# A fused attention and two feed-forward layers: weight sums at conversion, token forms on two engines, and a new order of copies in ScalarE's row

## The chip, the cores and the metric

The kernel runs on one core of a Trainium2 chip. What counts is the device time of one execution, in microseconds, as the median of several runs. A core has five engines that run side by side, each through a row of its own instructions in order: TensorE (PE; matmuls, with its weight loads shown as PEld), VectorE (DVE), ScalarE (ACT), GpSimd (POOL) and SyncE (SP), which only starts transfers here. They wait for each other through semaphores. Matmuls write to PSUM, a memory of eight banks of 128 x 512 numbers here; everything else lies in SBUF.

## What is computed

A decaying linear attention over blocks of 64 positions, then two feed-forward layers on 1536 tokens of width 512. In the reference:

```python
x = attn_out.transpose(0, 2, 1, 3).reshape(B * S, H * D)   # 1536 x 512
h = x @ w_in                                               # 512 -> 2048
g = np.where(h >= 1, h, np.where(h <= -1, 0.0, (h + 1) ** 2 / 4))
x = g @ w_out                                              # 2048 -> 512
gate = 1.0 / (1.0 + np.exp(-(x @ w_gate)))                 # 512 -> 1536
val = x @ w_val                                            # 512 -> 1536
return (gate * val @ w_out2).astype(np.float32)            # 1536 -> 512
```

Everything is float32. The weights come as 64-bit words.

## The kernel before

**Precision.** TensorE takes numbers of a shorter type (fp32r). So each operand is split in two, a high part and the rest, and each product is made of three matmuls: high times high, low times high, high times low. A split is a copy on ScalarE (to the short type) and a subtraction on VectorE (the rest).

**Stages.** Attention fills the first 80 us or so. Then comes the first layer: 16 slices of 128 hidden units, three blocks of 512 tokens. GROUPS cuts the 16 slices in groups (4, 3, 3, 3, 3); for a group, each block is taken in turn, and for each slice of the group there are 12 matmuls of `hidden` and 12 of `project`. A unit is one slice on one block. `feed_forward` issues the `project` of a unit two units later (LAG = 2). At a group's last slice `flush` (L239) adds the four banks of sums to `part[t]` on VectorE; after the last group it also splits the result into `xh` and `xl` (L247, L248), the tokens of the second layer.

**The second layer** has 12 slices, each with a gate and a value. For the first two token blocks, gate and value of a slice are 2 x 2 blocks of weights times tokens, and they are computed with 7 block products and not 8, as in Strassen's method. This needs sums of token blocks (token forms, `x_forms`) and sums of weight blocks (`w_forms`), which are then split too (L323 and L324 for tokens; `w_forms_split` with L346 on ScalarE and L347 on GpSimd for weights). The third token block is computed plainly by `single`. `pair_begin` and `pair_end` make the seven products of a slice (6 matmuls each, L357, in banks p0, p1, p2). p0 gathers several products one after the other: each time that its value is one of the results, ScalarE copies it out (L374, L378, L382), and the next product adds on top. The next product into p0 must wait for that copy.

**An iteration** of `second_layer` takes two slices n0 and n1 (GF = 2): the pair of n0 (its first five products, then the waiting projects of the last iteration, then its last two), the pair of n1, and the projects and singles: 204 matmuls, 180 in the first iteration, which has no waiting projects, while the last two projects come after the sixth.

**Weights.** Pieces of 128 x 512 weights come in by DMA and are converted by `w_round`, a pipeline of three steps for three pieces: words (L99, L100 on ScalarE), float (L106, L107, L109 on VectorE), high and low part (L113 on ScalarE, L117 on VectorE). NWP = 10 tiles hold converted pieces. `w_forms` of before takes high and low of two pieces, adds them to whole numbers (L335, two additions on GpSimd per slice), and makes four half-size sums (L339).

**What sets the order.** The program is written in the order in which each engine runs it. There is no scheduler that moves instructions: what stands earlier in the code on an engine runs earlier. Work for a later step, as conversions and splits, is called between the products. `later` is a list of splits that `finish` takes one at a time after a project. Tiles of a pool with n buffers are reused in turn; a write into a reused buffer waits for the last reader of its old content. `rest` tiles are r and q, `parts` makes gh and gl, the split of the activations (L185, L186).

Of the kernel before, what the change touches and what calls it, by code (L numbers as in the profile page):

```python
# [17 lines left out]
P = 128  # L18
# [7 lines left out]
GROUPS = (4, 3, 3, 3, 3)  # L26
GF = 2
# [11 lines left out]
def fused_kernel(ctx: ExitStack, tc: tile.TileContext, qkv, qd, cst, w1, w2, out):  # L39
# [9 lines left out]
    gp = ctx.enter_context(tc.tile_pool(name="gp", bufs=5))  # L49
# [28 lines left out]
    raws, ws, tmps = {}, {}, {}  # L78

# [14 lines left out]
    def w_words(i):  # L94
        word = raws[i].bitcast(U32).rearrange("p (n two) -> p n two", two=2)
        lo, hi = word[:, :, 0], word[:, :, 1]
        r = tp.tile([P, 512], F32, tag="r", bufs=3, name=f"wr{i}")
# [17 lines left out]
    def w_low(i, eng):  # L115
        r = tmps.pop(i)[1]
        eng.tensor_tensor(out=ws[i][:, 1], in0=r, in1=ws[i][:, 0].bitcast(F32), op=ALU.subtract)  # L117
# [3 lines left out]
    def w_round(eng=dve, between=None, low=dve):  # L121
        k = prog["round"]
# [17 lines left out]
        if 0 <= k - 2:  # L140
            w_low(k - 2, low)
        if eng is dve:
            w_load()
# [35 lines left out]
    def rest(name):  # L179
        return gp.tile([P, TT], F32, tag="r", name=name)  # L180
# [76 lines left out]
    def feed_forward(rounds):  # L257
# [14 lines left out]
        for u in seq:  # L272
# [14 lines left out]
            if n == NF1 - 1 and t == 1:  # L287
                w_need(NF1, 0)
                w_need(NF1, 512)
                w_forms(NF1)  # L290
                later.append(lambda: w_forms_split(NF1))
# [15 lines left out]
    forms = {}  # L307
    xt = {}

    def x_forms():  # L310
# [7 lines left out]
        for o, a, b_ in ((x1, y1, x1), (y1, y2, y1), (y2, y2, x1), (x2, x2, y2)):  # L318
            pool.tensor_tensor(out=o, in0=a, in1=b_, op=ALU.subtract)
# [6 lines left out]
        for i in (1, 0, 3, 2):  # L326
            later.append(lambda i=i: split(i))

    def w_forms(n):

        hw = HK * P
        v, g = f = [gv.tile([P, 512], F32, tag="gv", name=f"{c}{n}") for c in "vg"]
        for o, d in ((512, v), (0, g)):
            w = ws[index[n, o]]
            pool.tensor_tensor(out=d, in0=w[:, 0].bitcast(F32), in1=w[:, 1].bitcast(F32), op=ALU.add)  # L335
        v1, v2, g1, g2 = v[:, 0:hw], v[:, hw:], g[:, 0:hw], g[:, hw:]
        for o, a, b_, op in ((v2, v1, v2, ALU.add), (v1, g1, v1, ALU.subtract),
                             (g1, v2, g1, ALU.subtract), (g2, g2, g1, ALU.subtract)):
            pool.tensor_tensor(out=o, in0=a, in1=b_, op=op)  # L339
        forms[n] = f  # L340

    def w_forms_split(n):
        tiles = []
        for i, f in enumerate(forms[n]):
# [63 lines left out]
    def second_layer():  # L408
        waiting = []
        for n0 in range(NF1, NF1 + NF2, GF):  # L410
# [27 lines left out]
            if n2 < NF1 + NF2:  # L438
                w_forms_split(n2)
# [376 lines left out]
```

## Time and profile before

| | us |
| --- | --- |
| median of 3 runs | 683.87 |
| lowest and highest run | 683.08, 684.03 |
| the profiled execution, its time | 681.24 |
| span of the profiled execution | 679.5 |

| stage (us of the span) | length | matmuls in the program |
| --- | --- | --- |
| 80 to 319.64, first layer | 239.64 | 1057 records |
| 319.64 to 345.50, its end after the second block | 25.86 | 48 |
| 345.50 to 395.07, slices 16 and 17 | 49.57 | 180 |
| 395.07 to 447.94, slices 18 and 19 | 52.87 | 204 |
| 447.94 to 503.97, slices 20 and 21 | 56.03 | 204 |
| 503.97 to 560.91, slices 22 and 23 | 56.94 | 204 |
| 560.91 to 618.33, slices 24 and 25 | 57.42 | 204 |
| 618.33 to 675.19, slices 26 and 27, with the last two projects | 56.86 | 228 |

The profile is that of one execution, whose time is 2.63 us under the median. In its rows, a tile's name has its buffer number left out, `<-` reads as "made from", and a bracket at the end of a timeline row gives the idle time just before it and what ended it. PEclk is the clock that TensorE was granted, as a share of 2.4 GHz.

### The profile page before, as it was taken

To read this page: it belongs to the slowest core of one execution; us is meant where nothing else is said; L and a number is where in the kernel's file an instruction comes from. 1 tells how busy PE (TensorE), PEld (TensorE's weight loads), DVE (VectorE), ACT (ScalarE), POOL (GpSimd) and SP (SyncE) were. 2 spreads that over 40 slices of the span, in tenths; PEclk is the share of its full clock that TensorE was granted. 3 is DMA by queue.
4 is the path that set the end of the run, shared out by engine and by line. 5 is a ranking of instruction groups with operands and counts; after the bars stand their busy time and mean duration, and the time that the engine had idled before them with its cause. 6 is when DMAs were issued, how large, how long until landed. Compare 5 with 4: busy or idle time off the path is not lost.

```text
span 679.5 us, 8022 instructions
## 1 busy us (share of the span) xinstructions
PE 621.5 (91%) x3004; PEld 499.5 (74%) x3004; DVE 436.2 (64%) x699; ACT 329.7 (49%) x593; POOL 164.5 (24%) x158
## 2 busy tenths in 40 slices
PE   8889899999999999999478997996997899699897
PEld 5767688888888888888366876874876687488686
DVE  6665832676675685697786884596398279353344
ACT  6667644665564563655454564434353254222220
POOL 4367500000000000043904054052232405404100
PEclk8999899999999999999778998998999799699899
DMA  8965300132130121231021321132033012000013
GB/s 283 359 237 188 123 31 1 63 97 90 61 94 32 63 93 32 63 93 32 7 87 32 110 82 56 32 93 63 0 94 93 1 62 63 0 0 1 1 55 130
DMA packets 15813, 52.58 MB, mean 77 GB/s; under 512 B 1688, under 2 KB 2976, under 8 KB 15776
## 3 DMA queue, kind: packets, MB, share of 16 engines
q1 hardware_dynamic: 15760, 52.08, 23.3%
q8 instruction: 23, 0.38, 0.2%
q14 instruction: 14, 0.11, 0.0%
q10 hardware_dynamic: 16, 0.01, 0.0%
HBM read 48.92 MB, written 3.15 MB: 77 GB/s over the span
## 4 chain that ended last, share of the span: by engine, by line
PE 55%; issue 19%; POOL 10%; DVE 7%; ACT 6%; DMA 2%; SPq 1%; POOLq 0%
PE a L217 24%; PE h L163 8%; PE h L165 8%; PE h L164 8%; PE p L357 6%; POOL s L347 3%; POOL v L339 2%; POOL g L335 2%; POOL g L339 2%; DVE pT L630 1%; POOL v L335 1%; DMA u<-in_qkv 1%; ACT wr L99 1%; DVE xl L687 1%; DMA pd<-pw 1%
## 5 line engine op out<-in xcount | busy, mean ns | idle before, releaser
L217 PE MATMUL a<-gh,w 128*128 128x512 f32 x384 | 121.8, 399 | 5.1 <-ACT gh L185 5.1
L163 PE MATMUL h<-xh,w 128*128 128x512 f32 x288 | 112.6, 391 | 0.3 <-ACT xh L686 0.3
L165 PE MATMUL h<-xl,w 128*128 128x512 f32 x288 | 112.2, 390 | 0.0
L164 PE MATMUL h<-xh,w 128*128 128x512 f32 x288 | 112.2, 389 | 0.0
L217 PE MATMUL a<-w,gh 128*128 128x512 f32 x288 | 89.1, 391 | 1.2 <-DVE part L239 1.2
L217 PEld LDWEIGHTS a<-gh,w 128*128 128x128 f32 x384 | 74.2, 194 | 21.0 <-ACT gh L185 5.5
L217 PE MATMUL a<-gl,w 128*128 128x512 f32 x192 | 76.9, 401 | 5.0 <-DVE gl L186 5.0
L198 DVE SCALAR_TENSOR_TENSOR r<-r,h 128x512 f32<-128x512 f32 x48 | 32.9, 685 | 74.4 <-ACT r L194 74.4
L193 ACT ACTIVATE r<-h,half 128x512 f32<-128x512 f32 x48 | 33.1, 689 | 87.7 <-PE h L165 87.7
L239 DVE TENSOR_TENSOR part<-part,a 128x512 f32<-128x512 f32 x108 | 67.8, 680 | 7.3 <-PE a L217 7.3
L335 POOL TENSOR_TENSOR v<-w 128x512 f32<-128x512 f32 x12 | 17.5, 1458 | 215.1 <-DVE w L117 215.1
L347 POOL TENSOR_TENSOR s<-v,s 128x512 fp32r<-128x512 f32 x12 | 15.8, 1319 | 217.6 <-ACT s L346 144.5
L357 PE MATMUL p<-xth,s 128*128 128x512 f32 x96 | 40.3, 498 | 30.0 <-ACT q L374 25.5
L217 PEld LDWEIGHTS a<-w,gh 128*128 128x128 f32 x288 | 53.8, 188 | 13.8 <-DVE part L239 2.5
L163 PEld LDWEIGHTS h<-xh,w 128*128 128x128 f32 x288 | 54.1, 188 | 12.1 <-ACT xh L686 0.7
L165 PEld LDWEIGHTS h<-xl,w 128*128 128x128 f32 x288 | 54.0, 188 | 11.6 <-DVE xl L687 0.3
L164 PEld LDWEIGHTS h<-xh,w 128*128 128x128 f32 x288 | 54.1, 188 | 11.1
L185 ACT ACTIVATE gh<-r 128x512 fp32r<-128x512 f32 x60 | 37.5, 625 | 48.0 <-DVE r L403 35.5
L186 DVE TENSOR_TENSOR gl<-r,gh 128x512 fp32r<-128x512 f32 x60 | 43.0, 717 | 20.5 <-ACT gh L185 20.5
L217 PE MATMUL a<-w,gl 128*128 128x512 f32 x144 | 56.1, 389 | 0.0
L107 DVE SCALAR_TENSOR_TENSOR wr<-raw,wr 128x512 uint32<-128x512 uint32 x68 | 54.4, 799 | 2.3
L357 PEld LDWEIGHTS p<-xth,s 128*128 128x128 f32 x96 | 22.0, 234 | 41.2 <-ACT q L374 30.1
(97 smaller groups left out, 1083.1 us busy)
## 6 DMA issues: line engine op xcount, KB each, us to landing
raw<-in_w SPq DMA_DIRECT2D x68, 512.0 KB, 3.5
u<-in_qkv SPq DMA_DIRECT2D x12, 768.0 KB, 5.6
u<-in_qkv SPq DMA_DIRECT2D x8, 384.0 KB, 6.3
out<-part SPq DMA_DIRECT2D x12, 256.0 KB, 2.1
DT<-pd SPq DMA_DIRECT2D x1, 256.0 KB, 4.6
qp<-pd SPq DMA_DIRECT2D x2, 96.0 KB, 4.6
DT<-pd SPq DMA_DIRECT2D x1, 128.0 KB
cs<-in_cst SPq DMA_DIRECT2D x1, 98.0 KB, 2.0
```

The source lines that it names most:

```text
L107: dve.scalar_tensor_tensor(out=ru, in0=hi, scalar=0x80000000, in1=ru, op0=ALU.bitwise_and, op1=ALU.bitwise_or)
L163: pe.matmul(h, lhsT=wh, rhs=xh[:, k, tt], start=(k == 0), stop=False)
L164: pe.matmul(h, lhsT=wl, rhs=xh[:, k, tt], start=False, stop=False)
L165: pe.matmul(h, lhsT=wh, rhs=xl[:, k, tt], start=False, stop=(k == NP - 1))
L185: act.activation(gh, g, AF.Copy)
L186: dve.tensor_tensor(out=gl, in0=g, in1=gh.bitcast(F32), op=ALU.subtract)
L193: act.activation(r, h, AF.Relu, bias=half, scale=0.5)
L217: pe.matmul(accs[j], lhsT=a, rhs=b_, start=(first and m == 0), stop=(last and m == 2))
L239: dve.tensor_tensor(out=o, in0=o, in1=accs[j], op=ALU.add)
L335: pool.tensor_tensor(out=d, in0=w[:, 0].bitcast(F32), in1=w[:, 1].bitcast(F32), op=ALU.add)
L347: pool.tensor_tensor(out=t[:, 1], in0=f, in1=t[:, 0].bitcast(F32), op=ALU.subtract)
L357: pe.matmul(o, lhsT=a, rhs=b_, start=(start and k == 0 and m == 0), stop=(k == HK - 1 and m == 2), skip_group_check=True)
```

## The change

1. `w_forms` is called from `w_round` right behind the low part of a slice's second piece, and works in place on the whole numbers that the conversion has (tile r of `w_words`, now five buffers); the two additions L335 are not there any more. The forms are split in the next `w_round`, ScalarE and GpSimd as before. So a slice's forms are made and split a group ahead. The pool fp of split forms has four buffers, not three; the pool gv is gone.
2. `x_forms` makes two of the four token forms on VectorE and two on GpSimd, and the splits of two forms are in one step of `later`.
3. GROUPS is (4, 3, 3, 2, 4), and gh and gl have four buffers, not five.
4. A pair is a generator. The last two products of the first pair come behind the waiting projects as before; then each step of the second pair (up to its fifth product) comes with one step of the first pair's activation parts behind it, so the copies of the second pair's p0 stand ahead of the parts in ScalarE's row. The parts of the second pair stand between the two `hidden` of a `single`, the parts of a single behind the next project. `w_round` is called in front of each waiting project, eight times per iteration in all.

The diff, cut to its core:

```diff
-GROUPS = (4, 3, 3, 3, 3)
+GROUPS = (4, 3, 3, 2, 4)
...
+    def w_forms(i):
+        n, o = pieces[i]
         r = tmps.pop(i)[1]
+        whole[n, o] = r
+        if n < NF1 or o != 512:
+            return
+        hw = NP // 2 * P
+        v, g = whole.pop((n, 512)), whole.pop((n, 0))
+        v1, v2, g1, g2 = v[:, 0:hw], v[:, hw:], g[:, 0:hw], g[:, hw:]
+        for o, a, b_, op in ((v2, v1, v2, ALU.add), (v1, g1, v1, ALU.subtract),
+                             (g1, v2, g1, ALU.subtract), (g2, g2, g1, ALU.subtract)):
+            pool.tensor_tensor(out=o, in0=a, in1=b_, op=op)
+        forms[n] = v, g
...
     def w_round(eng=dve, between=None, low=dve):
+        split = [n for n in forms if n not in ready]
+        w_steps(eng, between, low)
+        for n in split:
+            w_forms_split(n)
+
+    def w_steps(eng, between, low):
...
             w_low(k - 2, low)
+            w_forms(k - 2)
...
-        for o, a, b_ in ((x1, y1, x1), (y1, y2, y1), (y2, y2, x1), (x2, x2, y2)):
-            pool.tensor_tensor(out=o, in0=a, in1=b_, op=ALU.subtract)
+        for eng, o, a, b_ in ((dve, x1, y1, x1), (pool, y1, y2, y1), (dve, y2, y2, x1),
+                              (pool, x2, x2, y2)):
+            eng.tensor_tensor(out=o, in0=a, in1=b_, op=ALU.subtract)
...
-        for i in (1, 0, 3, 2):
+        later.append(lambda: (split(0), split(1)))
+        later.append(lambda: None)
+        for i in (3, 2):
             later.append(lambda i=i: split(i))
...
+    def pair_act(n, r, gs):
+        hi, lo = ([gp.tile([P, TT], F32R, tag=c, name=f"{c}{n}_{t}") for t in range(2)]
+                  for c in ("gh", "gl"))
+        gs.update({t: (hi[t], lo[t]) for t in range(2)})
+        rest_of = lambda t: dve.tensor_tensor(out=lo[t], in0=r[t], in1=hi[t].bitcast(F32),
+                                              op=ALU.subtract)
+        act.activation(hi[0], r[0], AF.Copy)
+        yield
+        rest_of(0)
+        act.activation(r[1], r[1], AF.Sigmoid)
+        yield
+        dve.tensor_tensor(out=r[1], in0=r[1], in1=r[2], op=ALU.mult)
+        yield
+        act.activation(hi[1], r[1], AF.Copy)
+        yield
+        rest_of(1)
+        yield
...
-            a = pair_begin(n0)
-            w_need(n1, 0)
-            w_need(n1, 512)
-            w_forms(n1)
+            a, b = pair(n0), pair(n1)
+            for _ in range(5):
+                next(a)
             for p in waiting:
+                w_round()
                 project(*p)
-                w_round()
-            ga = pair_end(*a)
-            w_forms_split(n1)
-            w_round()
-            b = pair_begin(n1)
+            ra, ga = next(a), {}
+            xa = pair_act(n0, ra, ga)
+            for _ in range(5):
+                next(b)
+                next(xa)
             w_round()
             project(n0, 0, ga[0], True, False)
             w_round()
-            gb = pair_end(*b)
-            w_round()
-            ha = single(n0, 2)
+            rb, gb = next(b), {}
+            ha = single(n0, 2, pair_act(n1, rb, gb))
             w_round()
             project(n1, 0, gb[0], False, True)
...
+            ha = parts(ha, n0, 2)
             w_round()
             hb = single(n1, 2)
...
-    fp = ctx.enter_context(tc.tile_pool(name="fp", bufs=3, reuse_waits="tile"))
-    gv = ctx.enter_context(tc.tile_pool(name="gv", bufs=2, reuse_waits="tile"))
+    fp = ctx.enter_context(tc.tile_pool(name="fp", bufs=4, reuse_waits="tile"))
```

How the rows of the engines change is shown at three places. Names end in slice numbers (q20_1 is the copy 1 of slice 20; s22_1 a split form of slice 22) or in piece numbers (w52, wr54, raw54: pieces of weights; 50 and 51 are slice 22's). The first is ScalarE's row in the iteration of slices 20 and 21, between the two pairs. Before:

```order
L113 ACTIVATE w53_3933<-wr53_3813 128x512
L99 ACTIVATE wr55_3935<-raw55_3912 128x512
L100 ACTIVATE wc55_3936<-raw55_3912 128x512
L185 ACTIVATE gh20_0_3956<-q20_0_3839 128x512
L393 ACTIVATE q20_1_3840<-q20_1_3840 128x512
L185 ACTIVATE gh20_1_3962<-q20_1_3840 128x512
L346 ACTIVATE s21_0_3966<-v21_3878 128x512
L346 ACTIVATE s21_1_3969<-g21_3879 128x512
L374 ACTIVATE q21_0_3975<-p21_0_3972 128x512
L378 ACTIVATE q21_1_3976<-p21_0_3972 128x512
L379 ACTIVATE q21_0_3975<-q21_0_3975 128x512
```

In the kernel with the change, from the first pair's sigmoid on:

```order
L398 ACTIVATE q20_0_3830<-q20_0_3830 128x512
L140 ACTIVATE s22_0_3869<-wr51_3727 128x512
L140 ACTIVATE s22_1_3872<-wr50_3689 128x512
L114 ACTIVATE w52_3894<-wr52_3768 128x512
L100 ACTIVATE wr54_3896<-raw54_3825 128x512
L101 ACTIVATE wc54_3897<-raw54_3825 128x512
L385 ACTIVATE q21_0_3936<-p21_0_3933 128x512
L413 ACTIVATE gh20_0_3946<-q20_0_3830 128x512
L416 ACTIVATE q20_1_3831<-q20_1_3831 128x512
L391 ACTIVATE q21_1_3937<-p21_0_3933 128x512
L420 ACTIVATE gh20_1_3947<-q20_1_3831 128x512
```

The copies q21_0 and q21_1 stood behind gh20_0, gh20_1 and two splits; now q21_0 stands ahead of gh20_0 and q21_1 ahead of gh20_1, and the splits are those of slice 22, ahead of the conversion of w52 and the words of piece 54.

The second is VectorE's row at the same place, from the last flush addition of the waiting projects on. Before:

```order
L239 TENSOR_TENSOR part2_1014<-part2_1014,a18_2_3_3898 128x512
L106 TENSOR_SCALAR wr54_3907<-wr54_3907 128x512
L107 SCALAR_TENSOR_TENSOR wr54_3907<-raw54_3818,wr54_3907 128x512
L109 ISA wr54_3907<-wr54_3907,wc54_3908 128x1024
L117 TENSOR_TENSOR w53_3933<-wr53_3813,w53_3933 128x512
L390 TENSOR_TENSOR q20_0_3839<-q20_0_3839,p20_0_3836 128x512
L391 TENSOR_TENSOR q20_1_3840<-q20_1_3840,p20_2_3838 128x512
L186 TENSOR_TENSOR gl20_0_3957<-q20_0_3839,gh20_0_3956 128x512
L394 TENSOR_TENSOR q20_1_3840<-q20_1_3840,q20_2_3841 128x512
L186 TENSOR_TENSOR gl20_1_3963<-q20_1_3840,gh20_1_3962 128x512
L376 TENSOR_TENSOR q21_0_3975<-q21_0_3975,p21_1_3973 128x512
```

With the change:

```order
L272 TENSOR_TENSOR part2_1011<-part2_1011,a18_2_3_3887 128x512
L401 TENSOR_TENSOR q20_0_3830<-q20_0_3830,p20_0_3827 128x512
L403 TENSOR_TENSOR q20_1_3831<-q20_1_3831,p20_2_3829 128x512
L388 TENSOR_TENSOR q21_0_3936<-q21_0_3936,p21_1_3934 128x512
L411 TENSOR_TENSOR gl20_0_3948<-q20_0_3830,gh20_0_3946 128x512
L418 TENSOR_TENSOR q20_1_3831<-q20_1_3831,q20_2_3832 128x512
L397 TENSOR_TENSOR q21_2_3938<-q21_2_3938,p21_2_3935 128x512
L411 TENSOR_TENSOR gl20_1_3949<-q20_1_3831,gh20_1_3947 128x512
```

One conversion (of pieces 53 and 54) that stood between the flush and the multiplication into q20_0 is gone from here, and the first addition of slice 21 (q21_0) stands ahead of gl20_0.

The third is VectorE's row in the transition from the first layer to the second, from the last flush addition of the second token block on (part1). Before:

```order
L239 TENSOR_TENSOR part1_1013<-part1_1013,a13_1_3_2844 128x512
L248 TENSOR_TENSOR xl_77<-part1_1013,xh_76 128x512 x2
L324 TENSOR_TENSOR xtl_1016<-part1_1013,xth_1015 128x1024
L186 TENSOR_TENSOR gl14_2_2956<-r14_2_2912,gh14_2_2955 128x512
L198 SCALAR_TENSOR_TENSOR r15_2_2959<-r15_2_2959,h15_2_0_2942 128x512
L324 TENSOR_TENSOR xtl_1016<-part0_79,xth_1015 128x1024
L106 TENSOR_SCALAR wr37_2804<-wr37_2804 128x512
L107 SCALAR_TENSOR_TENSOR wr37_2804<-raw37_2752,wr37_2804 128x512
L109 ISA wr37_2804<-wr37_2804,wc37_2805 128x1024
L117 TENSOR_TENSOR w36_2984<-wr36_2747,w36_2984 128x512
L186 TENSOR_TENSOR gl15_2_2994<-r15_2_2959,gh15_2_2993 128x512
L324 TENSOR_TENSOR xl_77<-part1_1013,xh_76 128x2x512
```

With the change (L347 are the token forms, L352 their splits):

```order
L272 TENSOR_TENSOR part1_1010<-part1_1010,a12_1_3_2761 128x512
L281 TENSOR_TENSOR xl_77<-part1_1010,xh_76 128x512 x2
L347 TENSOR_TENSOR part0_79<-part1_1010,part0_79 128x1024
L347 TENSOR_TENSOR part1_1010<-part1_1010,part0_79 128x1024
L352 TENSOR_TENSOR xtl_1013<-part0_79,xth_1012 128x1024
L352 TENSOR_TENSOR xtl_1013<-part1_1010,xth_1012 128x1024
L219 TENSOR_TENSOR gl13_2_2894<-r13_2_2848,gh13_2_2893 128x512
L231 SCALAR_TENSOR_TENSOR r14_2_2897<-r14_2_2897,h14_2_0_2880 128x512
L107 TENSOR_SCALAR wr35_2633<-wr35_2633 128x512
L108 SCALAR_TENSOR_TENSOR wr35_2633<-raw35_2593,wr35_2633 128x512
L110 ISA wr35_2633<-wr35_2633,wc35_2634 128x1024
L118 TENSOR_TENSOR w34_2920<-wr34_2588,w34_2920 128x512
```

Two forms of 1024 columns came to VectorE, the two splits of the first forms stand ahead of gl13_2, and since the last group has four slices, one unit more follows.

## Rows read from the trace of the kernel before

**Rows 1.** The page's busy table: busy us, share of the span, instructions.
```profile
PE 621.5 (91%) x3004; PEld 499.5 (74%) x3004; DVE 436.2 (64%) x699; ACT 329.7 (49%) x593; POOL 164.5 (24%) x158
```

**Rows 2.** Windows by stage: length; busy us (instructions) per engine; PEclk, DMA share, GB/s.
```profile
80.00:319.64 239.64, 239.64 (x1057) 198.42 (x1056) 155.27 (x250) 134.01 (x227) 11.98 (x10) 1.00 0.20 64
319.64:345.50 25.86, 15.71 (x50) 11.56 (x49) 22.02 (x22) 10.37 (x16) 18.30 (x10) 0.77 0.12 33
345.50:395.07 49.57, 44.16 (x182) 35.17 (x181) 37.61 (x56) 30.23 (x52) 9.69 (x10) 0.95 0.24 71
395.07:447.94 52.87, 49.01 (x206) 39.26 (x204) 34.18 (x51) 24.35 (x44) 16.72 (x16) 0.97 0.19 57
447.94:503.97 56.03, 49.39 (x206) 39.21 (x205) 37.55 (x55) 22.86 (x41) 17.77 (x17) 0.94 0.19 57
503.97:560.91 56.94, 50.29 (x205) 39.86 (x204) 37.56 (x55) 22.84 (x41) 17.79 (x17) 0.94 0.18 56
560.91:618.33 57.42, 50.79 (x206) 40.26 (x205) 35.84 (x51) 19.01 (x33) 20.52 (x19) 0.91 0.06 19
618.33:675.19 56.86, 54.18 (x229) 43.68 (x227) 22.81 (x35) 11.80 (x20) 7.22 (x8) 0.97 0.11 39
```

The engines in these rows are PE, PEld, DVE, ACT and POOL, in this order.

**Rows 3.** Waits: engine, line <- releaser: us in total, times, longest.
```profile
PE p L357 <- ACT q L374: 25.5, 11, 5.0
```

**Rows 4.** Timeline between the pairs of slices 20 and 21: start, us, engine, line.
```profile
468.18 0.63 ACT L185 ACTIVATE gh<-q 128x512 fp32r<-128x512 f32 x1 [4.25 <-DVE q L390]
468.77 0.63 ACT L393 ACTIVATE q<-q 128x512 f32<-128x512 f32 x1
...
470.17 0.63 ACT L185 ACTIVATE gh<-q 128x512 fp32r<-128x512 f32 x1 [0.76 <-DVE q L394]
470.70 0.61 ACT L346 ACTIVATE s<-v 128x512 fp32r<-128x512 f32 x1
...
471.74 0.58 ACT L374 ACTIVATE q<-p 128x512 f32<-128x512 f32 x1
...
472.37 0.79 PE L357 MATMUL p<-xth,s 128*128 128x512 f32 x1 [5.05 <-ACT q L374]
...
473.94 0.79 PE L357 MATMUL p<-xth,s 128*128 128x512 f32 x1 [0.77 <-POOL s L347]
```

**Rows 5.** A window around that gap's end, columns as in rows 2.
```profile
470.20:477.00 6.80, 3.86 (x8) 2.77 (x9) 1.38 (x2) 2.64 (x6) 5.61 (x5) 0.50 0.01 2
```

**Rows 6.** Timeline of ScalarE, first pair of the last iteration.
```profile
619.94 0.60 ACT L374 ACTIVATE q<-p 128x512 f32<-128x512 f32 x1 [4.39 <-PE p L357]
```

**Rows 7.** Timeline of TensorE, first pair of slices 20 and 21.
```profile
451.23 0.73 PE L357 MATMUL p<-xth,s 128*128 128x512 f32 x2 [0.41 <-ACT q L374]
```

**Rows 8.** Timelines of the transition (GpSimd, TensorE, VectorE).
```profile
320.47 2.40 POOL L319 TENSOR_TENSOR part<-part,part 128x1024 f32<-128x1024 f32 x1 [3.17 <-DVE part L239]
...
330.35 1.22 PE L217 MATMUL a<-gh,w 128*128 128x512 f32 x2 [5.11 <-ACT gh L185]
...
344.46 2.47 DVE L239 TENSOR_TENSOR part<-part,a 128x512 f32<-128x512 f32 x4
...
349.26 1.22 DVE L324 TENSOR_TENSOR xtl<-part,xth 128x1024 fp32r<-128x1024 f32 x1
...
350.71 0.50 PE L357 MATMUL p<-xth,s 128*128 128x512 f32 x1 [1.49 <-ACT q L374]
```

**Rows 9.** Groups by form: count, busy us, mean ns, idle before.
```profile
L335 POOL TENSOR_TENSOR v<-w 128x512 f32<-128x512 f32 x12 | 17.5, 1458 | 215.1 <-DVE w L117 215.1
...
L100 ACT ACTIVATE wc<-raw 128x512 int32<-128x512 uint32 x68 | 44.9, 661 | 0.0
```

**Rows 10.** Timeline of VectorE: beside GpSimd's work (449.36) and without it.
```profile
449.36 1.52 DVE L106 TENSOR_SCALAR wr<-wr 128x512 uint32<-128x512 uint32 x1
...
460.19 0.42 DVE L106 TENSOR_SCALAR wr<-wr 128x512 uint32<-128x512 uint32 x1
...
461.98 0.68 DVE L117 TENSOR_TENSOR w<-wr,w 128x512 fp32r<-128x512 f32 x1
```

More of the change, by code (lines that the diff above doesn't have):

```diff
@@ L78, in fused_kernel @@
     raws, ws, tmps = {}, {}, {}
+    whole, forms, ready = {}, {}, {}
     prog = {"loaded": 0, "round": 0}
@@ L324, in split @@
             dve.tensor_tensor(out=lo, in0=f[i], in1=hi.bitcast(F32), op=ALU.subtract)
-        for i in (1, 0, 3, 2):
+        later.append(lambda: (split(0), split(1)))
+        later.append(lambda: None)
+        for i in (3, 2):
             later.append(lambda i=i: split(i))
[L329 to L344, printed above, removed]
-            t = fp.tile([P, 2, 512], F32R, tag="s", name=f"s{n}_{i}")
-            act.activation(t[:, 0], f, AF.Copy)
-            pool.tensor_tensor(out=t[:, 1], in0=f, in1=t[:, 0].bitcast(F32), op=ALU.subtract)
-            tiles.append(t)
-        forms[n] = tiles
     def product(o, w, c, x, start):
@@ L362, in x_at, with pair @@
         return xh[:, ks, tt], xl[:, ks, tt]
-    def pair_begin(n):
+    def pair(n):
         w_need(n, 0)
         w_need(n, 512)
+        if n not in ready:
+            w_forms_split(n)
         hw = HK * P
         g, v = ws[index[n, 0]], ws[index[n, 512]]
-        s31, s24 = forms.pop(n)
+        s31, s24 = ready[n]
         t_at = lambda i: (xt["h"][:, i], xt["l"][:, i])
@@ L383, in pair_begin, with single @@
         dve.tensor_tensor(out=r[2], in0=r[2], in1=p2, op=ALU.add)
-        return n, p0, p2, r, v, s24, t_at(2)
-    def pair_end(n, p0, p2, r, v, s24, t4):
-        hw = HK * P
-        product(p0, v, hw, t4, False)
+        act.activation(r[0], r[0], AF.Sigmoid)
+        yield
+        product(p0, v, hw, t_at(2), False)
+        dve.tensor_tensor(out=r[0], in0=r[0], in1=p0, op=ALU.mult)
         product(p2, s24, hw, x_at(1, 1), False)
-        dve.tensor_tensor(out=r[0], in0=r[0], in1=p0, op=ALU.mult)
         dve.tensor_tensor(out=r[1], in0=r[1], in1=p2, op=ALU.add)
-        gs = {0: parts(r[0], n, 0)}
+        yield r
+    def pair_act(n, r, gs):
[5 more added lines that the diff above has]
+        act.activation(hi[0], r[0], AF.Copy)
+        yield
+        rest_of(0)
         act.activation(r[1], r[1], AF.Sigmoid)
+        yield
         dve.tensor_tensor(out=r[1], in0=r[1], in1=r[2], op=ALU.mult)
-        gs[1] = parts(r[1], n, 1)
-        return gs
-    def single(n, t):
-        h, v = hidden(n, t, 0), hidden(n, t, 512)
+        yield
+        act.activation(hi[1], r[1], AF.Copy)
+        yield
+        rest_of(1)
+        yield
+    def single(n, t, between=()):
+        between = iter(between)
+        h = hidden(n, t, 0)
+        for _ in between:
+            pass
+        v = hidden(n, t, 512)
         used.update((index[n, 0], index[n, 512]))
@@ L403, in single @@
         dve.tensor_tensor(out=r, in0=r, in1=v, op=ALU.mult)
-        return parts(r, n, t)
+        return r
     def second_layer():
@@ L437, in second_layer @@
             w_round()
-            if n2 < NF1 + NF2:
-                w_forms_split(n2)
             project(n0, 1, ga[1], True, False)
-            w_round()
+            hb = parts(hb, n1, 2)
             project(n1, 1, gb[1], False, True)
```

34 lines of the change are left out of this document (16 added, 18 removed).

## The prediction

> **What bounds the kernel now.** I read the busy shares first, to find the engine that matters: TensorE is busy 91% of the span, GpSimd 24% [rows 1]. So the time is TensorE's work plus its gaps, and the question is where the gaps lie. The windows by stage give that [rows 2]. From 80 to 319.64 TensorE is busy all the time at a granted clock of 1.00: 1057 matmuls in 239.64 us, 0.2267 us each. That pitch is my ruler: a stage's loss is its length minus its matmuls times 0.2267. The counts are the program's (48, 180, four times 204, 228; the windows show one or two more, records at their edges). The stretch from 319.64 to the first pair loses 25.86 - 48 x 0.2267 = 14.98; the six iterations of the second layer lose 8.76, 6.62, 9.78, 10.69, 11.17 and 5.17. Together 67.2 us. The change can win little beyond that: it leaves the first 80 us nearly alone, and the next 240 have no gap.
>
> What ends the gaps? The table of waits puts 25.5 us in 11 waits on one line: TensorE's third product of a pair waits for ScalarE's copy L374 [rows 3]. The timeline of one of them shows why the copy is late [rows 4]. TensorE resumes at 472.37 after 5.05 us, so its second product ended at 467.3 and the data of the copy were there; the copy itself takes 0.58. But ScalarE runs its row in order, and ahead of L374 stand a gh that waits for VectorE's L390, a sigmoid, a second gh that waits for VectorE again, and two splits L346. After one matmul TensorE waits for GpSimd's s as well. Then the clock: 470.2 to 477.0 is granted at 0.50, the lower level of 1.2 GHz [rows 5]; the matmuls that end the gap run slow, and 6.8 us at half speed cost up to 3.4. The 10 to 11 us of a steady iteration are thus 5.1 for the copy, about 1 for GpSimd's s, 3 to 4 for the clock, the rest small pieces.
>
> A copy need not cost anything. In the last iteration ScalarE had idled 4.39 us, waiting for TensorE, and the copy starts at once [rows 6]. At the first pair of iteration 20/21, behind other work on ScalarE, it costs a gap of 0.41 [rows 7].
>
> In the transition [rows 8] GpSimd makes token forms of 1024 columns (the first 2.40 us), the parts for the last projects stand behind the splits of these forms, and TensorE idles 5.11 at 330.35 and more later. The first pair's third product starts at 350.71, 31.07 after the stretch begins, where 60 matmuls need 13.6.
>
> **The change part by part.** *Copies ahead.* In an iteration ScalarE's row now has a pair's copies ahead of the other pair's parts, so the 5.05 for L374 goes. What is late next? I follow the steady iteration 20/21, t = 0 at the first pair's first product, by pitch: five products to 6.8, two waiting projects to 12.24, products six and seven to 14.96, the second pair's first two to 17.68. New in ScalarE's row is the split of a group ahead: s22_1 takes the buffer of s20_1, which product seven reads last. So ScalarE stands until 14.96, and queued behind it are w52, two word copies, then copy q21_0. With 0.61 for a split [rows 4] and as much for w52, 0.66 for a word copy [rows 9], w52 ends at about 16.2, the words at 17.5, the copy at 18.1: TensorE, there at 17.68, loses about 0.5. On VectorE the low part of w52 starts at 16.3; behind it are the four flush additions of the waiting projects (2.47 for four, [rows 8]) and the multiplication into q20_0, each with a start after a wait; the bank that the fourth product of the second pair takes comes free at about 20.8, where TensorE is there at 19.5: 1.3. The second copy, behind gh20_0 and a sigmoid, is about 0.55 late. With 0.6 for the first pair's own copy, still behind two word copies (0.41 in rows 7), 0.3 of small pieces and 0 to 1.6 for a clock that may fall, I take 3.8 lost in each of the three steady iterations. Bounds: 2.5, if no gap drops the clock and covers are a little longer, and 6, if each drops it. In the second iteration no flush addition stands there (the sums are copied, not added): 1.5, from 0.8 to 3.5. The last has no next group: 0.5, from 0.3 to 1.5.
>
> *Sums at conversion.* Two additions L335 of 1.46 us per slice [rows 9] fall, 24 in all; four half-size sums and two splits per slice stay, earlier. GpSimd is felt on VectorE: the same L106 takes 1.52 beside GpSimd's work and 0.42 without it, where L117 takes 0.68 [rows 10]. A third less of it is a gain that I count at nothing, because the new place of the sums, right behind the low parts, lies beside VectorE's row again. VectorE's slack hides them in the steady iterations (37.55 of 56.03 us busy, [rows 2]); without that cover they would cost up to 2 each, inside the 6.
>
> *Transition.* GROUPS now ends in a group of four, so 72 matmuls (16.32 us) follow the last project of the second token block, not 48 (10.88), and this point comes 5.44 earlier, at 314.2. VectorE's row then sets the end: 2.0 until the flush is done, two xl, x1, a wait of 2.4 for y1 on GpSimd (the 2.40 of rows 8), y2, a wait of 2.4 for x2, two 1024-wide splits at 1.22 [rows 8], three gl and two clamps at about 0.7 (the size of L117), three weight rounds of 2.5 (0.42 + 3 x 0.68, [rows 10]), two more wide splits. That is 1.4 + 2.4 + 4.9 + 3.5 + 7.4 = 19.6 of work and 6.8 of waits. About 2.1 for GpSimd's sums of slice 17 beside it brings the flush of the third block to 28.5 (26.4 with none, 29.2 with more). Now it starts at 344.46, 24.8 into its stretch, and the third product follows 6.25 later (350.71). With 5.35 of the same work after it, since the wide split of rows 8 no longer stands there and the copy waits only for xl, a round and the words, I get 33.85 (31.7 to 34.5), so 348.05 against 350.71: 2.7 won. TensorE's own waits in the stretch are absorbed, because VectorE's row ends later. After the third product the first iteration now loses 6.3 (350.71 to 395.07 with 168 matmuls); I expect 3.5: 0.85 for a third copy, 1.5 to 3 for the clock, 0.3. Together 5.5 won: 23.74 lost becomes 18.2, from 15.5 to 24 (nothing won).
>
> The Trainium skill ("SBUF — State Buffer", Who interferes with whom) says that a VectorE instruction with two SBUF inputs and a GpSimd instruction that reads SBUF shut each other out for a whole instruction. The 1.52 against 0.42 of rows 10 agrees in size. It speaks against this change, whose token forms and sums run on both engines at once: if GpSimd's four sums and two splits for slice 17 (four at half of L335's 1.46, two at 1.4, 5.7 in all) stopped VectorE throughout, and not for the 2.1 that I took, the sum below would be 652.4.
>
> *Group of two.* One group of the first layer flushes per two units, not three. VectorE then has 0.7 + 0.7 + 2.5 per unit and half of 2.47, 5.1, against 5.44 of TensorE (24 matmuls). It fits; I count 0.5 (0 to 4, if GpSimd beside it takes it over 5.44). gh and gl have four buffers, not five; at a lag of two units no row then waits for one: nothing (a bound of 1).
>
> **Sum.** Lost after: 18.2 + 1.5 + 3 x 3.8 + 0.5 = 31.6, and 0.5 for the group of two. Against 67.2 that wins 35.1 us. The span 679.5 becomes 644.4, the profiled execution 681.24 becomes 646.1. The median of the runs shown, 683.87, is 2.63 above that execution; with it, **648.8**.
>
> **The rivals.** *Nearly all gaps go* (0.07). If the waits for buffers fall where TensorE has cover and the clock stays up: 10 for transition and first iteration, 1 for each of four, 0.3: 14.3, so 52.9 won, 631. For it: rows 6. Against it: VectorE's row alone is 26 us long in the transition.
>
> *Half of it comes back* (0.18). The split's buffer holds ScalarE and through it VectorE, the clock halves after each gap: 24 for transition and first iteration, 7 for each of four, 1.5, and 4 for the group of two: 57.5 lost, 9.7 won, 674. For it: rows 5. Against it: the gaps that I find are 0.5 to 1.3 long, not 5.
>
> *Slower* (0.03). One mechanism: from product seven on, s22_1's split, w52, its low part, four flush additions and q20_0's multiplication run in series, 0.6 + 0.6 + 0.7 + 2.5 + 0.7 = 5.1, before the second pair's bank is free. Slowed to twice by GpSimd and followed by half clock, an iteration loses 10: 24 + 5 x 10 + 4 = 78, 10.8 more than now, 695. It decides from 43/5 = 8.6 lost per iteration; against it stands the 4.5 us that TensorE has to do meanwhile.
>
> *The change doesn't do what it says* (0.02). The copies stand ahead in the row, but what they wait for comes later by as much: 683 to 685.
>
> **How the numbers follow.** The forecast, 640 to 664, has 0.70. Its low end: 15.5 + 0.8 + 3 x 2.5 + 0.3 = 24.1 lost, 43.1 won, 640.8. Its high end is not all upper bounds at once (24 + 3.5 + 18 + 1.5 + 4 = 51 lost, 667.7) but all save the group of two. Left out so far are 0.30, so the range goes on to 668 and takes in those bounds and the near part of the half gain, about 0.10. A measurement of this kernel can tell about 0.2% from no change. Faster by more: 0.70 + 0.07 + 0.18 = 0.95; within: 0.02; slower: 0.03.
>
> **What would show it.** Right: TensorE's waits for the first copy fall from 25.5 to under 8 in all; the steady iterations are about 50 us long (46.25 + 3.8) at a clock of 0.95 or more; a split in ScalarE's row waits for TensorE's seventh product; TensorE's next longest wait is for the bank that VectorE's multiplication frees; the first pair's third product starts some 34 us after the second block's last project, with VectorE's flush a little before it. Wrong: gaps of over 3 us in the second pair, gaps in the first layer around the group of two, clock 0.50 in each iteration, or VectorE's subtractions at 1.2 us and more all along.

## The result and the profile after

The changed kernel takes 642.1 us (641.25 to 642.64) against 683.48 (682.87 to 684.03) before: a ratio of 0.9394, 95% interval 0.9377 to 0.941. The forecast was 648.8, with a range of 640 to 668.

The busy table of the changed kernel's page has the same columns as rows 1:

```profile
span 640.5 us, 7949 instructions
PE 606.9 (95%) x3004; PEld 490.0 (77%) x3004; DVE 428.1 (67%) x701; ACT 328.6 (51%) x593; POOL 127.4 (20%) x132
```

TensorE's share rises from 91% to 95%, GpSimd has almost a quarter less to do. The windows by stage, as in rows 2 (length; PE, PEld, DVE, ACT, POOL; granted clock, DMA share, GB/s), begin at the changed kernel's own stages:

```profile
80.00:313.89 233.89, 233.89 (x1034) 193.72 (x1034) 147.81 (x240) 129.01 (x217) 7.54 (x8) 1.00 0.19 61
313.89:343.82 29.93, 19.89 (x74) 14.97 (x72) 27.12 (x33) 16.90 (x27) 13.54 (x8) 0.87 0.18 53
343.82:388.81 44.99, 44.30 (x181) 35.84 (x182) 32.39 (x48) 25.49 (x45) 11.01 (x11) 0.93 0.22 64
388.81:436.87 48.06, 47.09 (x206) 38.14 (x205) 37.62 (x57) 28.07 (x52) 15.96 (x14) 1.00 0.27 81
436.87:486.56 49.69, 47.71 (x206) 37.98 (x204) 37.97 (x58) 23.70 (x43) 11.47 (x12) 1.00 0.23 69
486.56:535.41 48.85, 47.48 (x205) 38.06 (x204) 35.24 (x55) 22.57 (x41) 11.55 (x12) 1.00 0.22 64
535.41:584.27 48.86, 47.46 (x206) 38.06 (x205) 33.44 (x51) 18.07 (x32) 11.55 (x12) 1.00 0.06 20
584.27:636.35 52.08, 52.08 (x229) 42.60 (x227) 22.81 (x35) 10.61 (x18) 0.00 (x0) 1.00 0.12 43
```

With the pitch of the prediction (0.2267 us; 72 matmuls in the second window, then 180, four times 204, 228) the losses are 13.6 and 4.2 where they were 15.0 and 8.8, then 1.8, 3.4, 2.6, 2.6 and 0.4 where they were 6.6, 9.8, 10.7, 11.2 and 5.2. Together 28.7 for 67.2. From the second iteration on the clock is at 1.00, where rows 2 had 0.91 to 0.97. An iteration without any gap measures 46.64, not 46.25, so 0.39 of each loss is the pitch of the second layer and no wait.

What the steady iterations still lose stands mostly between the two pairs. The timeline of the changed kernel there (ScalarE, VectorE and TensorE rows from separate answers):

```profile
445.79 0.63 ACT L140 ACTIVATE s<-wr 128x512 fp32r<-128x512 f32 x1
453.10 0.64 ACT L140 ACTIVATE s<-wr 128x512 fp32r<-128x512 f32 x1 [6.68 <-PE p L365]
453.64 0.62 ACT L114 ACTIVATE w<-wr 128x512 fp32r<-128x512 f32 x1
...
455.28 0.58 ACT L385 ACTIVATE q<-p 128x512 f32<-128x512 f32 x1
...
454.29 1.37 DVE L118 TENSOR_TENSOR w<-wr,w 128x512 fp32r<-128x512 f32 x1 [4.70 <-ACT w L114]
455.58 2.47 DVE L272 TENSOR_TENSOR part<-part,a 128x512 f32<-128x512 f32 x4
457.97 0.67 DVE L401 TENSOR_TENSOR q<-q,p 128x512 f32<-128x512 f32 x1
...
455.91 0.72 PE L365 MATMUL p<-xth,s 128*128 128x512 f32 x2 [0.16 <-ACT q L385]
458.70 0.73 PE L365 MATMUL p<-xth,s 128*128 128x512 f32 x2 [1.14 <-DVE q L401]
```

The second split stands 6.68 us until TensorE's seventh product has read the buffer. Behind it come w52's high part, then on VectorE its low part, the four flush additions and the multiplication L401, and TensorE waits 1.14 us for that one. The gap of 5.05 us of rows 4 has become one of 0.16 at the copy; TensorE's waits for the first copy fall from 25.5 us in 11 waits [rows 3] to 2.0 in 5:

```profile
PE p L365 <- DVE part L272: 5.7, 1, 5.7
PE p L365 <- DVE q L401: 3.4, 3, 1.1
...
PE p L365 <- ACT q L385: 2.0, 5, 1.0
```

(Waits: engine, line, releaser; us in all, times, longest.) The first row is new: at the end of the first layer the first pair's *first* product waits for VectorE's flush.

### The profile page after: what moved, and what is told of

It reads as the page before. It is cut to its first block, busy times and chain, and to the rows that moved or that the text cites. A ratio compares the mean times of both kernels' runs of the same rounds, so it can differ in the third digit from the quotient of the medians.

```text
span 640.5 us, 7949 instructions
## 1 busy us (share of the span) xinstructions
PE 606.9 (95%) x3004; PEld 490.0 (77%) x3004; DVE 428.1 (67%) x701; ACT 328.6 (51%) x593; POOL 127.4 (20%) x132
## 4 chain that ended last, share of the span: by engine, by line
PE 70%; DVE 16%; ACT 7%; DMA 3%; issue 3%; POOL 0%; SPq 0%; ACTq 0%; DVEq 0%
PE a L250 30%; PE p L365 15%; PE h L197 8%; PE h L198 8%; PE h L196 8%; DMA u<-in_qkv 3%; DVE part L272 2%; DVE w L118 2%; DVE pT L656 1%; DVE wr L108 1%; DVE wr L110 1%; ACT wr L100 1%; ACT wc L101 1%; DVE wr L107 1%; DVE xl L713 1%
## 5 line engine op out<-in xcount | busy, mean ns | idle before, releaser
L133 POOL TENSOR_TENSOR wr<-wr 128x256 f32<-128x256 f32 x24 | 19.8, 825 | 343.8 <-DVE w L118 342.9
L118 DVE TENSOR_TENSOR w<-wr,w 128x512 fp32r<-128x512 f32 x60 | 48.0, 801 | 15.5 <-ACT w L114 15.5
L114 ACT ACTIVATE w<-wr 128x512 fp32r<-128x512 f32 x68 | 42.3, 622 | 18.4 <-DVE wr L110 18.0
L108 DVE SCALAR_TENSOR_TENSOR wr<-raw,wr 128x512 uint32<-128x512 uint32 x68 | 50.0, 735 | 2.3
L110 DVE CUSTOM_DVE_ANT_0 wr<-wr,wc 128x1024 uint16<-128x1024 uint16 x59 | 45.2, 766 | 2.4
```

What stands on the lines that cost most here:

```text
L108: dve.scalar_tensor_tensor(out=ru, in0=hi, scalar=0x80000000, in1=ru, op0=ALU.bitwise_and, op1=ALU.bitwise_or)
L110: eng.tensor_tensor(out=ri, in0=ri, in1=c, op=ALU.add)
L114: act.activation(ws[i][:, 0], tmps[i][1], AF.Copy)
```

## The experiments

Each kernel is the changed one with one edit, unless it says otherwise; the edits are cut to their core. Losses are counted as above, from each trace. The kernel before, timed again with each group of experiments, had medians of 682.2 to 683.5 us, so a difference of about 1 us from the changed kernel tells little by itself.

**One: parts ahead of copies again.**

```diff
-            for _ in range(5):
-                next(b)
-                next(xa)
+            for _ in range(5):
+                next(xa)
+            for _ in range(5):
+                next(b)
```

> The changed kernel (642.1) with one part undone: all activation parts of a pair stand ahead of the next pair's copies in ScalarE's row again. My theory, that the copies' order is the bulk of the gain: between the pairs the copy q21_0 then comes behind gh20_0 (458.7 in the changed kernel's trace), a sigmoid and gh20_1 (to 461.7), so TensorE idles about 6 us where it idled 0.2 and 1.1, and the clock falls to half after it for about 3 more: 7 more lost in each of the three steady iterations, 2 to 5 in the first, second and last. About 675 us, and the wait of the third product for the copy back at 25 us or more in all. The rival, that earlier sums and less GpSimd work carry the gain, expects at most 10 us more: 652 or less.

Measured: 662.38 us (661.95 to 663.31), 20 more than the changed kernel and 13 less than expected. TensorE's row in a steady iteration:

```profile
461.87 1.22 PE L365 MATMUL p<-xth,s 128*128 128x512 f32 x2 [6.09 <-ACT q L385]
```

The steady iterations lose 9.4, 8.8 and 8.6 and their windows' granted clock is 0.94: the gap of 6 us is back, as expected, and the half clock after it (0.58 was granted from 461.8 to 468). But the first, second and last iterations lose only 3.9, 2.4 and 1.2, against 4.2, 1.8 and 0.4. There no split and no flush stands ahead of the copy, and the parts alone fit into TensorE's cover. So the order of copies and parts costs something only where other work makes the parts late. My expected 2 to 5 for those three iterations was wrong. The rival (10 us at most) falls too.

This kernel is still 20 us faster than the one before. Next to rows 2, the first, second and last iterations keep their gain (3.9, 2.4 and 1.2 for 8.8, 6.6 and 5.2), the steady ones little (9.4, 8.8 and 8.6 for 9.8, 10.7 and 11.2). The two splits that stood between the parts and the copy in rows 4 are gone from there, and the rounds of weights have other places; which of these brings the 20 us no run separates.

**Two: sums at their old place**, with the two additions per slice and the old buffers (fp 3, gv 2, conversion 3), copies ahead.

```diff
-            w_forms(k - 2)
...
+        v, g = [gv.tile([P, 512], F32, tag="gv", name=f"{c}{n}") for c in "vg"]
+        for o, d in ((512, v), (0, g)):
+            wt = ws[index[n, o]]
+            pool.tensor_tensor(out=d, in0=wt[:, 0].bitcast(F32), in1=wt[:, 1].bitcast(F32), op=ALU.add)
...
             for _ in range(5):
                 next(a)
+            w_need(n1, 0)
+            w_need(n1, 512)
+            w_forms(n1)
...
             ra, ga = next(a), {}
+            w_forms_split(n1)
```

> The changed kernel with the weight sums back at their old places: two additions per slice of high and low part on GpSimd, the sums within the group, the old buffers; copies stay ahead. My theory: the sums' place is worth little by itself, since GpSimd makes them early enough and no split then waits for product seven; the waits for the second pair's bank go, VectorE beside GpSimd is slower. 643 us, between 637 and 650. The rival, that conversion-time sums are half of the gain, expects 655 to 662.

Measured: 633.58 us (632.72 to 634.43), 8.5 *less* than the changed kernel, outside what either theory gave. From the second iteration on there is no gap at all. Its windows, columns as above:

```profile
388.89:435.53 46.64, 46.64 (x206) 38.30 (x204) 40.62 (x59) 28.61 (x52) 19.87 (x17) 1.00 0.31 92
435.53:482.17 46.64, 46.64 (x206) 38.30 (x204) 36.95 (x55) 23.11 (x41) 19.25 (x17) 1.00 0.23 68
```

GpSimd is busy 19.25 us of 46.64 in a steady iteration, where the changed kernel has 11.47 of 49.69. ScalarE's row shows why less work was slower: here both splits run one behind the other at 447.0, and nothing waits for product seven.

```profile
447.00 0.62 ACT L136 ACTIVATE s<-v 128x512 fp32r<-128x512 f32 x1
447.52 0.61 ACT L136 ACTIVATE s<-g 128x512 fp32r<-128x512 f32 x1
452.25 0.60 ACT L382 ACTIVATE q<-p 128x512 f32<-128x512 f32 x1 [4.11 <-PE p L362]
```

The copy L382 waits for TensorE, not TensorE for the copy. So in this order the sums at conversion are a loss.

**Three: the groups of before.**

```diff
-GROUPS = (4, 3, 3, 2, 4)
+GROUPS = (4, 3, 3, 3, 3)
```

> The changed kernel with the groups of the first layer as before (4, 3, 3, 3, 3). Theory: the stretch after the second block's last project starts 5.44 us later, but VectorE has one gl, one clamp and one weight round (3.9 us) less in it, so its flush of the third block comes 1.6 us later: 643.7 us. The rival, that the longer cover of 24 matmuls matters to TensorE by itself, expects 647 (all of 5.44).

Measured: 642.27 us (640.51 to 642.66): no difference that can be told. Transition and first iteration lose 17.7 together, against 17.8. The 1.6 that I expected isn't there: what the longer cover gives, one unit's work more on VectorE takes. But the waits stand at other places. With the old groups the first pair's first product starts while the flush still runs, and the third waits for the copy; in the changed kernel the first product waits for the flush. TensorE's rows (the flush beside the first), then that of the changed kernel:

```profile
342.54 0.61 PE L365 MATMUL p<-xh,w 128*128 128x512 f32 x2
341.59 2.48 DVE L272 TENSOR_TENSOR part<-part,a 128x512 f32<-128x512 f32 x4
347.85 1.22 PE L365 MATMUL p<-xth,s 128*128 128x512 f32 x2 [2.43 <-ACT q L385]
```

```profile
343.82 1.22 PE L365 MATMUL p<-xh,w 128*128 128x512 f32 x2 [5.74 <-DVE part L272]
```

**Four: all token forms on GpSimd.**

```diff
-        for eng, o, a, b_ in ((dve, x1, y1, x1), (pool, y1, y2, y1), (dve, y2, y2, x1),
+        for eng, o, a, b_ in ((pool, x1, y1, x1), (pool, y1, y2, y1), (pool, y2, y2, x1),
```

> The changed kernel with all four token forms on GpSimd. Theory: the chain of forms is 2 x (2.40 - 1.22) = 2.4 us longer, and VectorE, which waits for it, has 2.4 us less work: its flush of the third block comes 0 to 2.4 us later. 643.5 us. The rival, that forms on VectorE are what freed the transition, expects 647 or more; the other rival, that they burden VectorE, which is the bound there, expects less than 641.

Measured: 644.77 us (644.53 to 645.16), 2.7 more. The trace doesn't let me put that down to the forms: transition and first iteration lose 17.3, against 17.8, and all stages 28.1 against 28.7, while the last group's third block begins 1.9 us later (315.81, not 313.89), behind stages that this edit leaves alone. In experiments one and five to eight, whose edits leave them alone too, that block begins between 314.07 and 315.55, so most of the 1.9 is what those stages vary by from trace to trace.

**Five: the second split one round later**, so that it isn't ahead of w52 in ScalarE's row.

```diff
-        split = [n for n in forms if n not in ready]
+        split = [n for n in forms if len(ready.get(n, ())) < 2]
...
-        for i, f in enumerate(forms[n]):
+        for i in [len(tiles)]:
+            f = forms[n][i]
```

> The changed kernel with one step moved: of the two split forms of a slice the second is made one weight round later, so ScalarE's row has no split that waits for TensorE's seventh product ahead of w52, the words and the copy q21_0. Theory: that wait (6.68 us on ScalarE) is what makes TensorE lose 0.4 + 1.3 + 0.4 us between the pairs; all three go in the three steady iterations, 5 to 6 us in all: 636.5 us, and the steady iterations 47 us long. Rival: VectorE's row (37.97 of 49.69 us busy) is late by itself and the flush additions come no earlier: 641 or more.

Measured: 640.89 us (640.46 to 641.54): 1.2 less, not 5.6, and hardly clear of the noise. The mechanism is right where it was aimed, and the gain is lost elsewhere:

```profile
387.82:440.56 52.74, 48.48 (x206) 39.36 (x205) 38.73 (x56) 29.58 (x54) 16.12 (x15) 0.97 0.23 68
488.74:535.38 46.64, 46.64 (x206) 38.29 (x205) 35.99 (x55) 22.70 (x42) 12.24 (x12) 1.00 0.23 68
```

The fourth and fifth iterations are without a gap (2.6 lost each before the edit), so the split's wait for product seven was what held the row. The second iteration loses 6.5, against 1.8. Two rows tell it:

```profile
389.07 0.66 ACT L100 ACTIVATE wr<-raw 128x512 f32<-128x512 f32 x1 [5.66 <-POOL s L142]
...
394.96 1.08 PE L365 MATMUL p<-xth,s 128*128 128x512 f32 x2 [4.26 <-ACT q L385]
```

A word copy waits 5.66 us for a conversion buffer that still holds a sum, until GpSimd's split L142 has read it. Behind the word copy stands the pair's copy L385, and TensorE waits 4.26 for that.

**Six: the flush ahead of the last token split and round.**

```diff
         while behind:
-            finish()
+            project(*behind.pop(0))
         while later:
             later.pop(0)()
+        w_round()
```

> The changed kernel with one place changed: at the end of the first layer the last projects are issued together, and the last token split and one weight round come behind the flush of the third block (one round less there). Theory: VectorE's row is what the first pair's first product waits for (5.74 us); without 1.76 + 0.96 + 1.10 + 1.09 + 1.75 ahead of it the flush starts when the last project ends, at 337.9 and not at 341.9, the gap shrinks to about 2 and the clock falls for a shorter time or not at all: 4 to 6 us less, 637 us. Rival: ScalarE's copies of the tokens and the first copy q16_0 are next, and TensorE waits the same time two products later: 641 or more.

Measured: 641.75 us (637.69 to 642.62), not to be told from the changed kernel; the runs spread over 5 us, and the trace is that of the slowest. In it the transition loses 8.0 for 13.6, as expected (the first pair starts 4 us earlier, though the third block begins 1.7 later), but the first iteration 5.8 for 4.2 and the second 5.8 for 1.8. In the second the first pair's third product waits 2.76 us for a copy behind two splits that wait for GpSimd's sums (0.72 and 1.37). Again it is the sums in the conversion's row.

**Seven: both moves.**

> Both moves, the second split a round later and the flush ahead of the last token split: if they are independent, the sum of both, about 631.5 us. If one of them only shifts a wait to the other's place, 636 or more.

Measured: 636.25 us (635.35 to 637.19): transition 8.0, second iteration 6.7, fourth on 0.4. That is 5.9 less, where the two edits alone took 1.2 and 0.4. The wait in the second iteration that each brings comes only once with both: 6.5 and 5.8 were lost there with one edit, 6.7 with the two.

**Eight: two more GpSimd additions per slice**, in front of the sums at conversion.

```diff
         v, g = whole.pop((n, 512)), whole.pop((n, 0))
+        for o, d in ((512, v), (0, g)):
+            wt = ws[index[n, o]]
+            pool.tensor_tensor(out=d, in0=wt[:, 0].bitcast(F32), in1=wt[:, 1].bitcast(F32), op=ALU.add)
```

> The changed kernel with the two additions per slice put back on GpSimd, at conversion (they make the same whole numbers again): GpSimd has 2.9 us more per slice, 35 us in all, nothing else moves. Theory, as predicted: GpSimd's work is hidden by slack on VectorE and by ScalarE's own wait of 6.68 us; 642 to 645. Rival: contention with VectorE costs 2 us per iteration and the later split holds ScalarE: 655.

Measured: 658.11 us (658.03 to 658.8), 16 more. My theory falls: the work on GpSimd is not hidden at this place. Iterations two to five lose 11.2, 6.0, 4.7 and 4.7. The worst place is the second iteration's start:

```profile
392.14 0.63 ACT L143 ACTIVATE s<-wr 128x512 fp32r<-128x512 f32 x1 [3.94 <-POOL wr L136]
394.07 0.63 ACT L143 ACTIVATE s<-wr 128x512 fp32r<-128x512 f32 x1 [1.30 <-POOL wr L136]
...
397.70 0.59 ACT L388 ACTIVATE q<-p 128x512 f32<-128x512 f32 x1
...
398.35 1.22 PE L368 MATMUL p<-xth,s 128*128 128x512 f32 x2 [6.26 <-ACT q L388]
```

The splits in ScalarE's row wait for GpSimd's sums, with the pair's copy behind them. In experiment two the same additions are done before ScalarE's row comes to the splits, and cost nothing. The rival's number was near (655), and one of its two causes, the split that holds ScalarE, is what the rows show. For the other, contention with VectorE, they show no difference: in a steady iteration the subtraction behind the splits, beside GpSimd's, takes 1.81 us, and 1.83 in the changed kernel.

**Nine: the new order alone, in the kernel before.** Experiment two, with old groups, all forms on GpSimd and their splits one at a time, and five buffers for gh and gl.

```diff
-GROUPS = (4, 3, 3, 2, 4)
+GROUPS = (4, 3, 3, 3, 3)
...
-        later.append(lambda: (split(0), split(1)))
-        later.append(lambda: None)
-        for i in (3, 2):
+        for i in (1, 0, 3, 2):
             later.append(lambda i=i: split(i))
```

> The kernel before with the new order of a pair, its parts and the rounds of weights alone: sums at their old place on GpSimd with the two additions, four token forms on GpSimd one split at a time, old groups, old buffers. Theory, from the runs so far (groups and token forms changed nothing that can be told, sums at conversion cost 8.5): this one part carries the whole gain and more, 634 to 637 us, with no loss in the iterations after the first. Rival: groups and token forms only work together, and the 6 us won in the transition and first iteration need them: 640 us.

Measured: 635.75 us (634.63 to 637.74), ratio 0.9311 (0.9284 to 0.9339). Without the other three parts the order (copies, parts and rounds of weights together) takes 47 us off, more than the whole change. The transition loses 15.0 as before, the first iteration 4.1, every other 0.4.

**Ten and eleven: from experiment two on to a faster kernel.** Ten has the edit of six; eleven, besides, makes the forms later:

```diff
+        form(dve, x1, y1, x1)
+        form(pool, y1, y2, y1)
+        later.append(lambda: None)
+        later.append(lambda: (form(dve, y2, y2, x1), form(pool, x2, x2, y2), split(0)))
+        later.append(lambda: (split(1), split(3)))
+        later.append(lambda: split(2))
...
```

> The kernel with the sums at their old place (633.6) and with the flush of the third block ahead of the last token split and round of weights. Theory: the flush came 4 us earlier in the two runs with this move, but they lost it again in the second iteration, where a word copy waits for a buffer of whole numbers that GpSimd's split holds; with the sums in tiles of their own that wait can't be, so it stays won: 628 us, no loss over 0.6 in the second iteration. Rival: the missing round of weights itself makes the second iteration late: 632 to 634.

> The kernel of the run above with the token forms and splits later too: after the flush of the second block only x1 (VectorE) and y1 (GpSimd), then gl of the waiting unit, and the other forms and splits behind the next projects. Theory: VectorE's row no longer stands 2.5 us for y1 and its gl no longer behind two wide splits of 4.5 us, so the two gaps of 1.55 and 2.70 at the third block's projects go, and with them the half clock after them: 624 us. Rival: the same VectorE work is only moved to where the last gl and the flush wait for it: 627 to 629.

Ten: 628.57 us (628.11 to 629.58), ratio 0.9208 (0.9183 to 0.9233); transition 8.0, first iteration 3.1, second 0.6, third 1.2. With the sums in tiles of their own the earlier flush stays won, as the theory said. Eleven: 627.73 (627.0 to 630.98), not to be told from ten. The wait for gl only moved, so its rival holds. Of ten, then of eleven:

```profile
324.06 0.73 PE L242 MATMUL a<-gh,w 128*128 128x512 f32 x2 [1.55 <-ACT gh L210]
327.49 0.79 PE L242 MATMUL a<-gl,w 128*128 128x512 f32 x1 [2.70 <-DVE gl L211]
```

```profile
329.24 0.50 PE L242 MATMUL a<-gl,w 128*128 128x512 f32 x1 [3.51 <-DVE gl L211]
335.10 0.50 PE L242 MATMUL a<-gl,w 128*128 128x512 f32 x1 [1.50 <-DVE gl L211]
```

Both beat the changed kernel by some 14 us.

## Why the prediction was right, and where its steps were off

**The bound and the gap.** That the gap at L374 with its half clock was what could be won is shown by experiment nine: the order alone removes every gap from the second iteration on. Which of its moves does how much is shown for the copies in the changed kernel alone (experiment one: 20 us).

**The steady iterations** were costed at 3.8, from 0.5 at the copy, 1.3 at the bank, 0.55 at the second copy, 0.6 at the first pair's copy, 0.3, and 0 to 1.6 for the clock. The trace has 0.43, 1.42 and 0.37 lost at the first three of these places; the first pair's copy costs 0.85 in the third iteration and nothing in the next two; the clock nothing. So 3.4, 2.6 and 2.6. The chain from the split's buffer through w52 and the flush to the multiplication was read off the two rows of order, and its end, TensorE's start behind the bank, held to some 0.2 us. The first pair's copy and the clock were too dear by 2.8 in all. The second iteration (1.5) measured 1.8, the last (0.5) 0.4.

**Transition and first iteration**: 18.2 expected, 17.8 measured. That the sum came so near is luck: up to the third product I had 14.8 lost (33.85 less 84 matmuls) and 16.2 were, after it I had 3.5 and 1.6 were. The flush was expected 28.5 into the stretch and starts at 28.0 (341.89). I then let the third product wait for the copy. In fact the first product waited, 5.74 us, for the flush, the clock fell (0.52 from 344 to 350), and the third product came at 349.10, not 348.05. The 3.5 for the rest of the iteration was 1.6, because the clock loss sat ahead of it. What I left out is which banks the first pair gets. In the kernel before its first product starts without a wait:

```profile
345.50 1.06 PE L357 MATMUL p<-xh,w 128*128 128x512 f32 x2
```

The flush there runs from 344.46 to 346.93 [rows 8]. Experiment three, with the old groups, has no wait there either, and its third product waits for the copy as I had let it. So the group of four brought the wait to the first product, at no cost in the sum. That the banks come round in another order with it, so that the first pair begins in one that the flush frees, is my reading of these waits; the banks themselves stand in no row.

**Sums at conversion** were counted at nothing. By themselves they were not: experiment two puts them, with their splits and buffers, at 8.5 us in this order, as a cost. My sum had most of that cost, since the split's wait is in the 3.8, but under the copies' heading and without saying that the old place would avoid it. And GpSimd's time beside them is no small matter there (experiment eight, 16 us), through ScalarE's row and not through VectorE's slack. The Trainium skill's rule on VectorE and GpSimd shutting each other out ("SBUF — State Buffer", Who interferes with whom) is seen in the rows: the low part L118 takes 1.37 us at 454.29 beside a GpSimd split, where rows 10 have 0.68. The 1.52 against 0.42 that I set beside the rule is of an instruction with one input, not two. In the changed kernel's steady iterations L118 stands in the chain that ends in TensorE's wait of 1.14, so up to 0.7 of each such wait is its price there, an estimate from these rows. It need not cost anything: experiment two has GpSimd busy 8 us longer per iteration and no gap. The 652.4 that I worked out for VectorE stopped throughout did not come; the flush of the third block began no later than I had it.

**Group of two and token forms** were to bring 2.7 in the transition and cost 0.5. Their bound was right: the first layer has no gap, and experiment three finds nothing for the groups. The forms have no clear price (experiment four). Experiment nine, without both, loses 19.1 in transition and first iteration, against 17.8: by that, the other three parts brought about 1.3 of the 5.9 us won there.

**The sum.** 648.8 against 642.1 is 6.7 too high. 2.9 of it are losses (31.6 expected, 28.7 measured), 0.8 is the first layer, which got 0.3 shorter to the same point where I had 0.5 longer (less than that point varies by from trace to trace). The rest is the step from the profiled execution to the median: I added 2.63, and the changed kernel's profiled execution (642.59) lies 0.5 above its median. That is 3.1 of the error, more than any term of the sum.

**The rivals.** Slower and no change are refuted, half the gain too: no steady iteration had a gap over 1.2. The full gain (631) was not reached by this kernel. Experiments two and nine come within 5 us of it, ten and eleven below it. Their later iterations have no gap, or next to none, as that rival has it, but because the splits no longer wait for product seven, and not because such a wait found cover. The 8.6 from which I let the slower rival decide leaves out the 4 us that its own sum has for the group of two; with them it is 7.8, and the five iterations lost 0.4 to 3.4.

## What to carry to other kernels

When an engine's row holds a copy that the next matmul waits for, look not only at what stands ahead of it but at what each of those instructions waits for: a split made a group early, in a buffer still being read, held the row for 6.7 us, and the same splits made later cost nothing (experiment two). Removing work from an engine off the path is worth only what its results' readers wait for; here a kernel with 24 additions more was 8.5 us faster. Two cures of one gap need not add up (the order alone won 47 us, the order with the other parts 41), so measure each part alone before keeping both.

## What the runs showed of the hardware

TensorE's clock fell to the lower level (1.2 GHz) after the longer gaps and stayed up after the shorter ones: 0.52 to 0.58 was granted in the microseconds after gaps of 5.74 (the changed kernel) and 6.09 (experiment one), and 0.53 from 345.3 to 348.7 in experiment six after one of 2.45, but 1.00 in experiment seven after one of 1.92 and in the changed kernel's steady iterations with their gaps of up to 1.14. Two gaps close together, 1.61 and 1.07 in the last iteration of the kernel before, were also followed by slow matmuls (0.50 from 640.8 to 643.4). What decides between the cases no run here settles. I had allowed up to 1.6 us per steady iteration for it.
